# How the rows of w2 are split, how the last two output tiles are summed, and where scratch products stand, in a gated attention and MLP mix

## The chip, the core and the metric

The kernel runs on one core of a Trainium2 chip. The metric is the device time of one execution in microseconds (us), lower is better.

## What is computed

```python
def _A_ref(x, wqkv, wo):            # 16 heads of 28, S = 2048, D = 448
    qkv = ...                       # x @ wqkv, split into q, k, v
    idx = pos[:, None] - off[None, :]          # 8 keys: own position and 2, 4 .. 14 before
    logits = jnp.einsum("bhsd,bhswd->bhsw", q, kg) * scale
    attn = _softmax(masked logits, axis=-1)
    o = jnp.einsum("bhsw,bhswd->bhsd", attn, vg)
    return o.reshape(B, S, D) @ wo
def _B_ref(x, w1, b1, w2, b2):      # 448 -> 1792 -> 448, squared ReLU
    h = x @ w1 + b1
    r = jnp.where(h > 0, h, 0)
    return (r * r) @ w2 + b2
g = _sigmoid((x * gate_w).sum(-1, keepdims=True))
return g * a + (1 - g) * b
```

Everything is float32.

## The kernel before

**Precision.** TensorE (PE) works on a rounded 32-bit type. Every operand is therefore split into a high part (ScalarE, ACT, copies it into the rounded type) and a low part (VectorE, DVE, subtracts the high part from the raw value). Each product is the sum of three: high by high, high by low, low by high.

**Half rows.** The inner size 448 is 3 x 128 + 64. `side_by_side` issues products in pairs: one on rows 0 to 63 of the array, one on rows 64 to 127, for two different accumulators that lie in two PSUM banks. To sum all 128 rows of an operand, each accumulator first gets one half and later the other (`wo_first` and `wo_second`, `h_first` and `h_second`, `o_part` with `second`). Between the two, a tiny ACT instruction (`touch`, L702) makes sure that the first half has left PE. `qkv_first` (L403) is an exception: there the first products use all 128 rows, one slice k of x and wq at a time, for four token tiles.

**Stages.** (1) q, k and v for four chunks of 512 tokens, to 105 us. (2) The MLP in 28 turns of a loop over `g`: each computes two hidden tiles of 128 for one chunk (`h_first`, `h_turn`, `h_second`, `mlp_ops`) and adds the two hidden tiles before to the four token tiles' outputs (`o_part`). (3) The attention runs meanwhile on GpSimd (POOL: products, L506 and L518) and DVE (reductions, L510 and L528). (4) The heads' outputs times `wo`: pairs of token tiles, `wo_split` and then `wo_first` and `wo_second`; four pairs lie between the turns, four at the end, the last three of them in the final loop over `n`. `fin_add` (L991) takes an accumulator times its gate into the output tile and stores it (L995).

**Order of work.** Nothing is scheduled at run time. The order on ACT, DVE, POOL and SP (which issues the transfers) is written by a small planner (`Plan`): each job has a cost, dependencies and a priority, and is emitted when its turn comes in the plan's own time `plan.t`, which PE's products push on. START, FIRST, `plan.wire`, `plan.free` and the like set the plan's clock to the opening, which is written by hand. Accumulators in PSUM come from two rings of four, "m" (hidden tiles, attention outputs, copies of rows) and "b" (the MLP's outputs). `Acc` takes a place from a ring, and a later job gives it back.

**Rows of w2 and wo.** Rows 0 to 6 of w2 (128 x 448 each) are brought in before the loop. `row` loads the others and wo's: raw row to SBUF (L1109), high part on ACT (L1115). For the low part there are two ways. With `direct` DVE subtracts from the raw row in SBUF (L1117; the planner marks this job as using the port that DVE and POOL share). Without it the row waits in `rows_in` until `row_split` copies it with ACT into a PSUM bank of ring "m" (L1131) and DVE subtracts from there (L1133). Rows 7 to 10 go the first way, rows 11 to 13 and wo's the second, at most one in a turn.

**Scratch products.** `keep_warm(n)` (L774) issues n products of a zero tile into a bank that nobody reads: 16 ahead of everything, and after the first and second slices of `qkv_first` FILL[k] = 2 and 1 more.

Of the kernel before, what the change touches and what calls it, by code (L numbers as in the profile page):

```python
# [13 lines left out]
S, D, H, DH, W, F = 2048, 448, 16, 28, 8, 1792  # L14
P = 128
# [7 lines left out]
CH = 512  # L23
# [7 lines left out]
MM448, MM512 = 200.0, 226.7  # L31
PE_LAT = 175.0
LAT = 60.0
START = 4500.0
ORDER = (3, 0, 1, 2)
WARM = 16
FIRST = (3100.0, 2600.0, 2500.0)
FILL = (2, 1, 0)
PP_BUFS = 4
ST_BUFS = 3  # L40
BT_BUFS = 8
# [13 lines left out]
class Plan:  # L55
# [124 lines left out]
def gated_mix_kernel(ctx: ExitStack, tc: tile.TileContext, xT, wqkv, w1, w2, wo, b1, b2, out):  # L180
    nc = tc.nc

    def f32(ap):
        return ap.bitcast(F32)
# [60 lines left out]
    def dma(fn, packets, size, *deps, prio=MID, at=0.0):  # L245
        return add(SYNC, 430.0, fn, *deps, prio=prio, at=at, move=(packets, size))
# [147 lines left out]
    def qkv_first(x):  # L394
        four = range(4)
        q = accs(0, 0, four, "bbbb")
        for k in range(3):
            todo = [full(x, q[i], i, 0, (k,)) for i in four]
            for some in ((0, 1), (2, 3)) if k == 0 else (four,):
                for j in range(3):  # L400
                    for i in some:
                        acc, a, w, *_ = todo[i][j]
                        nc.tensor.matmul(acc.pt[:, :NQ], a, w, start=k == j == 0, stop=False)  # L403
            plan.pe(FIRST[k])
            keep_warm(FILL[k])
        for acc in q:
            acc.todo = 3
        k = accs(0, 1, four, "mmmm")
        t = [sum((last(x, a[i], i, b) for i in four), []) for b, a in ((0, q), (1, k))]
        f = [full(x, k[i], i, 1) for i in four]  # L410
        run(0, [t[0] + f[0] + f[1] + f[2] + f[3], t[1] + f[2] + f[3] + f[0] + f[1]],
            [(3, [(0, 0, q[0])], (k[0], k[0])),
             (12, [(0, i, q[i]) for i in (1, 2, 3)], (k[1], k[1])),
             (24, [], (k[0], k[2])), (33, [], (k[1], k[3])),
             (39, [(1, 0, k[0]), (1, 2, k[2])]), (48, [(1, 1, k[1]), (1, 3, k[3])])])
# [290 lines left out]
    def go(todo):  # L706
        side_by_side(*todo)
# [61 lines left out]
    nc.vector.memset(f32(zero), 0.0)  # L769
    nc.vector.memset(none, 0.0)  # L770

    def keep_warm(n):
        for _ in range(n):
            nc.tensor.matmul(warm[:, :2 * P].rearrange("p (i n) -> p i n", i=2), zero,  # L774
                             zero[:, None].to_broadcast([P, 2, P]), start=True, stop=True)

    keep_warm(WARM)

    raws = [rawp.tile([P, 4, 512], F32, tag="raw", name="wqraw0")]
    rx = rawp.tile([P, 4, 512], F32, tag="raw", name="xraw0")  # L780
    for cols in (slice(0, 256), slice(256, CH)):
        nc.scalar.dma_start(rx[:, 0, cols], xT[0, :, 0, cols])
    for k in range(4):
        if k < 3:
# [13 lines left out]
    x = X(x_tiles(0, xap))  # L798
    for k in range(3):
        nc.scalar.activation(wqh[:, k, :NQ], raws[0][:, k, :NQ], AF.Copy)  # L800
        for n, cols in enumerate((slice(0, 256), slice(256, CH)) if k == 0 else (slice(0, CH),)):
            if k or n:
                nc.scalar.activation(x.h[k][:, cols], rx[:, k, cols], AF.Copy)
            else:
                nc.vector.tensor_copy(x.h[k][:, cols], rx[:, k, cols])
            if not n:
                nc.vector.tensor_sub(wql[:, k, :NQ], raws[0][:, k, :NQ], f32(wqh[:, k, :NQ]))
            nc.vector.tensor_sub(x.l[k][:, cols], rx[:, k, cols], f32(x.h[k][:, cols]))
# [3 lines left out]
    nc.vector.tensor_sub(x.x8, rx[:, 3], f32(x.x7))  # L812


    plan.t, plan.wire = START, 17500.0
    plan.now = 10500.0
    plan.free.update({ACT: 11290.0, DVE: 11950.0, POOL: 1400.0, SYNC: 10500.0})
    raw_free[0] = raw_free[1] = [event(12000.0)]

    def wq_split(b, k):  # L820
        at = (11500.0, 13000.0)[b - 1]
# [7 lines left out]
    for k in range(4):  # L829
# [3 lines left out]
    xl = {1: x_load(1, 0), 2: x_load(2, 1)}  # L833
    w1_piece(1, None)
    x_bring(1, *xl[1], spill=False)
    x_stored[0] = [dma(lambda j=j, x=x: nc.sync.dma_start(x_d[0, j], f32(x.t[j])), 128, 4096, event(11950.0), prio=MID)
                   for j in range(4)]
    w1_piece(2, None)
    w1_piece(0, 0)
# [239 lines left out]
    def wo_three(acc, oh, ol, wh, wl, js):  # L1079
        return [(acc, oh, wh, js[0]), (acc, oh, wl, js[1]), (acc, ol, wh)]  # L1080

    def wo_full(st, r, ks):
        return sum((wo_three(st.accs[r], st.oh[:, k, r], st.ol[:, k, r], woh[:, k], wol[:, k], wo_jobs[k]) for k in ks), [])

    def wo_first(st):
        need(*st.jobs)
        go([wo_three(st.accs[r], st.o7, st.o8, wo7h, wo7l, wo_jobs[3]) + wo_full(st, r, (0, 1, 2)) for r in range(2)])
        j = touch(woh[:, 2, 0:1], plan.after_pe())
        for a in st.accs:
            a.rows, a.after = None, (j,)  # L1090

    def wo_second(st):
        go([wo_full(st, 1 - r, (2, 0, 1)) for r in range(2)])
        part_last[st.place] = [plan.after_pe()]
        for r in range(2):
            fin_add(st.par, st.t + r, st.accs[r], gt[:, st.par, st.t + r:st.t + r + 1])
# [43 lines left out]
    def w2_row(f):  # L1140
        name = f"w2raw{f}"
        row_low[name] = event()
        w2_jobs[f] = (row(name, w2[:, f], *w2hl(f), direct=f < NFA + 4), row_low[name])

    def wo_row(k):
        name = f"woraw{k}"
# [25 lines left out]
    def is_done(*jobs):  # L1172
        return all(plan.end(j) is not None and plan.end(j) < plan.t for j in jobs)
# [10 lines left out]
    for g in range(2, 2 * NF):  # L1184
        i, f = g // (NF // 2), g % (NF // 2) * 2
        c = ORDER[i]
        pc, pf = (c, f - 2) if f else (ORDER[i - 1], NF - 2)
        ends = f == NF - 2 and i < 3
        last = g == 2 * NF - 1
        if not f:  # L1190
            x, slots = X([nxt[j][0] for j in range(4)]), [nxt[j][1] for j in range(4)]
            x.parts = [(nxt[j][2], nxt[j][2]) for j in range(4)]
            nxt = {}
        if ends:
            plan.calm = plan.t + 21 * MM512 + 12 * MM448
        accs = h_first(x, c, f)
        if todo_rows:
            todo_rows.pop(0)()
        if f == 2 and 0 < i < 3:
            x_reload(i + 1, 3, free)  # L1200
        if ends:
            x_reload(i + 1, 0, slots[3])
        if last:
            wo_take(True)
        elif not todo_rows and not rows_in and len(wo_todo) + len(wo_loaded) > 4 and not wo_ready:
            wo_take()
        if f in (NF - 4, NF - 2):
            for tl in both:
                fin_fetch(c // 2, (c % 2) * 4 + tl)
        h_turn(accs, f)  # L1210
        if rows_in and is_done(rows_in[0][2]):
            row_split(*rows_in.pop(0))
        if g == 2:
            o_all(c, 0, True)
            del hs[c, 0], hs[c, 1]
        for tls in (left, right)[:1 if ends else 2]:
            o_part(pc, pf, False, tls)
        o_turn(pc, pf, left if ends else both)
        if f in (NF - 6, NF - 4):
            for tl in left if f == NF - 6 else right:  # L1220
                fin_begin(c // 2, (c % 2) * 4 + tl)
        h_second(x, accs, f)
        mlp_ops(accs, c, f)
        if ends:
            x_reload(i + 1, 1, slots[2])
            x_reload(i + 1, 2, slots[0])
            free = slots[1]
            o_part(pc, pf, False, right)
            o_turn(pc, pf, right)
        st = at_hand() if last or wo_ready else None  # L1230
        if st:
            wo_first(st)
            if last:
                wo_take(True)
        o_all(pc, pf, True)
        del hs[pc, pf], hs[pc, pf + 1]
        if st:
            wo_second(st)

    for n, (tls, second) in enumerate(((left, False), (right, False), (left, True), (right, True))):  # L1240
        if second:
            o_turn(c, f, tls)
        if n in (1, 2, 3):
# [51 lines left out]
```

## Time and profile before

| | |
|---|---|
| median of 3 runs | 416.26 us (416.22 to 418.59) |
| the profiled execution's own time | 417.06 us |
| its span, first to last instruction | 415.3 us |
| granted TensorE clock, mean | 0.998 |
| busy PE / DVE / ACT / POOL | 98% / 63% / 49% / 65% |
| moved by DMA | 73.75 MB, 178 GB/s on average |

Times in the views are microseconds from the start of the span. A row of the timeline has start, length, engine, line, operation, output and inputs, shape, the number of instructions that were merged in it, and, if the engine was idle before, for how long and what ended it. A row of a group has minimum, median and maximum of one instruction in ns. PE is matmul, PEld the loading of its weights, SPq the queue of SP. Matmuls overlap: one of 448 columns is shown 0.36 us long, but the next starts 0.2 us after it.

### The profile page before, as it was taken

The numbers are of one execution on the slowest core, as the hardware profiler recorded it, in microseconds if no ns is written. First come the engines' busy times: TensorE is split into PE (matmuls) and PEld (weight loads), VectorE is DVE, ScalarE is ACT, GpSimd is POOL, SyncE is SP. The second block draws the span as 40 slices with busy tenths as digits, with TensorE's granted clock in tenths as the row PEclk, the third lists the DMA queues.
The fourth block names the chain that finished last, engine by engine and source line by source line (L and its number), as shares of the span: only waits on it lengthen the run. The fifth ranks groups of instructions, "written<-read, shape, count | busy, mean of one in ns | idle before, by whom it ended". The sixth has DMA issues, their size and how long they took to land.

```text
span 415.3 us, 9283 instructions
## 1 busy us (share of the span) xinstructions
PE 408.8 (98%) x3847; PEld 376.7 (91%) x3847; DVE 263.3 (63%) x346; ACT 203.8 (49%) x497; POOL 270.2 (65%) x165
## 2 busy tenths in 40 slices
PE   8999999999999999999999999999999999999995
PEld 7999999999999988888888888988898888888994
DVE  4424422761486997877655998787786586493453
ACT  5657765332464655444455533543473343346730
POOL 0000000984989899989999897999899876950000
PEclk9999999999999999999999999999999999999999
DMA  7989999937164405544113668554626222057604
GB/s 235 393 285 318 371 367 357 377 112 252 46 219 182 149 11 226 208 142 170 38 48 127 203 149 291 160 138 138 194 70 220 108 86 83 1 148 156 144 2 177
DMA packets 64553, 73.75 MB, mean 178 GB/s; under 512 B 32320, under 2 KB 57344, under 8 KB 64128
## 3 DMA queue, kind: packets, MB, share of 16 engines
q1 hardware_dynamic: 64224, 72.90, 53.6%
q8 instruction: 30, 0.49, 0.5%
q10 hardware_dynamic: 288, 0.26, 0.2%
q14 instruction: 11, 0.09, 0.1%
HBM read 45.71 MB, written 28.25 MB: 178 GB/s over the span
## 4 chain that ended last, share of the span: by engine, by line
PE 94%; DVE 2%; issue 1%; DMA 1%; ACT 1%; DVEq 0%
PE b L316 30%; PE h L316 30%; PE qkv L316 23%; PE a L316 8%; PE qkv L403 2%; DMA wqraw<-wqkv 1%; DVE o L528 1%; DVE h L759 1%; DVE lg L510 0%; DVE w2bl L1117 0%; DVE bt_b L991 0%; ACT h L755 0%; ACT h L757 0%; DVEq L1290 0%; ACT wqh L800 0%
## 5 line engine op out<-in xcount | busy, mean ns | idle before, releaser
L506 POOL TENSOR_TENSOR pp<-q,k 128x896 f32<-128x896 f32 x64 | 139.1, 2208 | 83.4 <-DMA k<-k_d 77.5
L518 POOL TENSOR_TENSOR pp<-lg,v 128x896 f32<-128x896 f32 x64 | 119.4, 1959 | 5.4 <-DVE lg L510 4.6
L316 PE MATMUL qkv<-wqh,x 64*128 64x448 f32 (+1 forms) x528 | 91.6, 362 | 0.0
L510 DVE TENSOR_REDUCE lg<-pp 128x32 f32<-128x896 f32 x64 | 67.7, 1076 | 17.9 <-POOL pp L506 17.9
L316 PE MATMUL qkv<-wql,x 64*128 64x448 f32 (+1 forms) x264 | 75.2, 362 | 0.0
L316 PEld LDWEIGHTS qkv<-wqh,x 64*128 64x128 f32 x528 | 74.0, 184 | 0.3
L759 DVE TENSOR_TENSOR h<-h,h 128x512 fp32r<-128x512 f32 x56 | 38.6, 690 | 54.4 <-ACT h L758 53.7
L316 PE MATMUL b<-w2ah,h 64*128 64x448 f32 x448 | 69.2, 359 | 0.0
L528 DVE TENSOR_REDUCE o<-pp 128x112 f32<-128x896 f32 x64 | 67.1, 1067 | 2.1 <-POOL pp L518 2.1
L316 PE MATMUL b<-w2bh,h 64*128 64x448 f32 x448 | 66.8, 360 | 0.6 <-DVE h L759 0.6
L755 ACT ACTIVATE h<-h,b1z 128x512 f32<-128x512 f32 x56 | 36.6, 654 | 40.1 <-PE h L316 40.1
L316 PEld LDWEIGHTS b<-w2ah,h 64*128 64x128 f32 x448 | 47.2, 184 | 2.8
L316 PE MATMUL b<-w2al,h 64*128 64x448 f32 x224 | 46.9, 358 | 0.0
L316 PEld LDWEIGHTS b<-w2bh,h 64*128 64x128 f32 x448 | 42.1, 184 | 4.5 <-DVE h L759 0.9
L316 PEld LDWEIGHTS qkv<-wql,x 64*128 64x128 f32 x264 | 44.7, 184 | 0.2
L316 PE MATMUL b<-w2bl,h 64*128 64x448 f32 x224 | 40.7, 358 | 0.0
L338 ACT ACTIVATE st<-qkv 128x448 f32<-128x448 f32 x48 | 24.3, 539 | 22.8 <-PE qkv L316 15.5
L702 ACT ACTIVATE w1h<-w1h 128x2 fp32r<-128x2 f32 x28 | 5.8, 207 | 58.9 <-PE h L316 58.9
L757 ACT ACTIVATE h<-h 128x512 fp32r<-128x512 f32 x56 | 33.4, 596 | 1.5
L758 ACT ACTIVATE h<-h 128x512 f32<-128x512 f32 x56 | 33.2, 593 | 0.0
L316 PE MATMUL h<-x,w1h 64*128 64x512 f32 x168 | 33.0, 386 | 0.0
L316 PE MATMUL h<-x0b,w1h 64*128 64x512 f32 x168 | 28.1, 386 | 0.0
(129 smaller groups left out, 726.5 us busy)
## 6 DMA issues: line engine op xcount, KB each, us to landing
k<-k_d SPq DMA_DIRECT2D x8, 840.0 KB, 6.4
v<-v_d SPq DMA_DIRECT2D x8, 840.0 KB, 5.4
x_d<-x SPq DMA_DIRECT2D x12, 512.0 KB, 7.0
q_d<-st SPq DMA_DIRECT2D x8, 448.0 KB, 4.8
k_d<-st SPq DMA_DIRECT2D x8, 448.0 KB, 4.0
v_d<-st SPq DMA_DIRECT2D x8, 448.0 KB, 4.5
q<-q_d SPq DMA_DIRECT2D x8, 448.0 KB, 3.8
o_d<-o SPq DMA_DIRECT2D x16, 224.0 KB, 2.4
```

Of the source, the lines that this page charges most:

```text
L316: nc.tensor.matmul(acc.pt[:, :acc.n], a[rows], w[rows], start=acc.todo == acc.all, stop=acc.todo == 1)
L338: nc.scalar.activation(st[0][:, :, t % 2], pt[:, :D].rearrange("p (g c) -> p g c", g=G), AF.Copy)
L403: nc.tensor.matmul(acc.pt[:, :NQ], a, w, start=k == j == 0, stop=False)
L506: nc.gpsimd.tensor_mul(pr.rearrange("p (w c) -> p w c", w=W), q[:, s:s + 1].to_broadcast([P, W, C]), k[:, s:s + W])
L510: nc.vector.tensor_reduce(lgs[i][:, s], pr.rearrange("p (w h d) -> p w h d", w=W, h=HG), axis=AX.X, op=ALU.add)
L518: nc.gpsimd.tensor_mul(pr.rearrange("p (h d w) -> p w h d", h=HG, w=W), lgs[i][:, s][:, :, :, None].to_broadcast([P, W, HG, DH]), vs[i][:, ...
L528: nc.vector.tensor_reduce(o_t[par, s][:, g * C:(g + 1) * C], pr.rearrange("p (c w) -> p c w", w=W), axis=AX.X, op=ALU.add)
L702: return add(ACT, 205.0, lambda: nc.scalar.activation(ap, f32(ap), AF.Copy), *deps, prio=TURN)
L755: a = add(ACT, 656.0, lambda pt=pt, r=r: nc.scalar.activation(pt, pt, AF.Relu, bias=b1t[:, f + r:f + r + 1]), ready, bias_job[0], prio=NEXT)
L757: b = add(ACT, 600.0, lambda pt=pt, hh=hh: nc.scalar.activation(hh, pt, AF.Square), a, prio=NEXT)
L758: a = add(ACT, 600.0, lambda pt=pt: nc.scalar.activation(pt, pt, AF.Square), b, prio=NEXT)
L759: low = add(DVE, 690.0, lambda pt=pt, hh=hh, hl=hl: nc.vector.tensor_sub(hl, pt, f32(hh)), a, prio=NEXT)
```

## The change

All of w2's rows 7 to 13 now go by way of a PSUM copy. A turn of the loop may split two rows instead of one, and at g == 3 it splits two whether or not the plan has their high parts done. For the last pair of output tiles, `wo_first` sums only the 64-row slice (`wo7h`, `wo7l`), the MLP's part follows, and the new `wo_end` sums the three full slices with all 128 rows, all nine products of the first tile, its `fin_add`, then all nine of the second. The scratch products between the slices of `qkv_first` are gone, 18 instead of 16 stand ahead, and the plan's constants for the opening are set anew.

```diff
-START = 4500.0
+START = 4900.0
-WARM = 16
-FIRST = (3100.0, 2600.0, 2500.0)
-FILL = (2, 1, 0)
+WARM = 18
+FIRST = (2700.0, 2450.0, 2400.0)
...
             plan.pe(FIRST[k])
-            keep_warm(FILL[k])
...
-    keep_warm(WARM)
+    for _ in range(WARM):
+        nc.tensor.matmul(warm[:, :2 * P].rearrange("p (i n) -> p i n", i=2), zero,
+                         zero[:, None].to_broadcast([P, 2, P]), start=True, stop=True)
...
-    plan.t, plan.wire = START, 17500.0
-    plan.now = 10500.0
-    plan.free.update({ACT: 11290.0, DVE: 11950.0, POOL: 1400.0, SYNC: 10500.0})
-    raw_free[0] = raw_free[1] = [event(12000.0)]
+    plan.t, plan.wire = START, 15000.0
+    plan.now = 9800.0
+    plan.free.update({ACT: 10700.0, DVE: 11400.0, POOL: 1400.0, SYNC: 9800.0})
+    raw_free[0] = raw_free[1] = [event(11500.0)]
...
-    ... event(11950.0), prio=MID)          # stores of x_d[0, j]
+    ... event(11500.0), prio=MID)
...
-    def wo_first(st):
+    def wo_first(st, ks=(0, 1, 2)):
         need(*st.jobs)
-        go([wo_three(st.accs[r], st.o7, st.o8, wo7h, wo7l, wo_jobs[3]) + wo_full(st, r, (0, 1, 2)) for r in range(2)])
+        if not ks:
+            for a in st.accs:
+                a.all = a.todo = 12
+        go([wo_three(st.accs[r], st.o7, st.o8, wo7h, wo7l, wo_jobs[3]) + wo_full(st, r, ks) for r in range(2)])
...
+    def wo_end(st):
+        for r in range(2):
+            for e in wo_full(st, r, (0, 1, 2)):
+                acc, a, w, *js = e
+                need(*acc.after, *js)
+                nc.tensor.matmul(acc.pt[:, :D], a, w, start=False, stop=acc.todo == 1)
+                acc.todo, acc.after = acc.todo - 1, ()
+                plan.pe(MM448)
+            fin_add(st.par, st.t + r, acc, gt[:, st.par, st.t + r:st.t + r + 1])
...
-        w2_jobs[f] = (row(name, w2[:, f], *w2hl(f), direct=f < NFA + 4), row_low[name])
+        w2_jobs[f] = (row(name, w2[:, f], *w2hl(f), direct=False), row_low[name])
...
-        if rows_in and is_done(rows_in[0][2]):
-            row_split(*rows_in.pop(0))
+        for _ in range(2):
+            if rows_in and (g == 3 or is_done(rows_in[0][2])):
+                row_split(*rows_in.pop(0))
...
-            wo_first(st)
+            wo_first(st, (0, 1, 2) if n < 3 else ())
         o_part(c, f, second, tls)
-        if n in (1, 2, 3):
+        if n in (1, 2):
             wo_second(st)
+    wo_end(st)
```

More of the change, by code (lines that the diff above doesn't have):

```diff
@@ L770, in gated_mix_kernel @@
     nc.vector.memset(none, 0.0)
[L772 to L775, printed above, removed]
-    keep_warm(WARM)
+    for _ in range(WARM):
+        nc.tensor.matmul(warm[:, :2 * P].rearrange("p (i n) -> p i n", i=2), zero,
+                         zero[:, None].to_broadcast([P, 2, P]), start=True, stop=True)
     raws = [rawp.tile([P, 4, 512], F32, tag="raw", name="wqraw0")]
     rx = rawp.tile([P, 4, 512], F32, tag="raw", name="xraw0")
-    for cols in (slice(0, 256), slice(256, CH)):
+    halves = slice(0, 256), slice(256, CH)
+    for cols in halves:
         nc.scalar.dma_start(rx[:, 0, cols], xT[0, :, 0, cols])
@@ L800, in gated_mix_kernel @@
         nc.scalar.activation(wqh[:, k, :NQ], raws[0][:, k, :NQ], AF.Copy)
-        for n, cols in enumerate((slice(0, 256), slice(256, CH)) if k == 0 else (slice(0, CH),)):
+        for n, cols in enumerate(halves if k == 0 else (slice(0, CH),)):
             if k or n:
@@ L835, in gated_mix_kernel @@
     x_bring(1, *xl[1], spill=False)
-    x_stored[0] = [dma(lambda j=j, x=x: nc.sync.dma_start(x_d[0, j], f32(x.t[j])), 128, 4096, event(11950.0), prio=MID)
+    x_stored[0] = [dma(lambda j=j, x=x: nc.sync.dma_start(x_d[0, j], f32(x.t[j])), 128, 4096, event(11500.0), prio=MID)
                    for j in range(4)]
```

## The prediction, made before the changed kernel ran

> **What bounds the kernel now.** I read the page first, then the waits of PE, then the timeline around each place where PE is not full.
>
> ```profile
> span 415.3 us, 9283 instructions
> PE 408.8 (98%) x3847; PEld 376.7 (91%) x3847; DVE 263.3 (63%) x346; ACT 203.8 (49%) x497; POOL 270.2 (65%) x165
> PE warm L774 <- DVE b1z L770: 1.1, 1, 1.1
> PE b L316 <- DVE h L759: 0.6, 1, 0.6
> PE qkv L403 <- ACT wqh L800: 0.3, 1, 0.3
> ```
>
> The span is PE's: 408.8 of 415.3 us. The three last rows are all the waits of PE: one before its first instruction, one before the first real product, one in the MLP. Outside them an edit can move the time only if it takes instructions out of PE's stream, or shortens what follows PE's last product. So there are three places to price: the opening, the one stall in the middle, the end.
>
> **The opening: scratch products.** The list shows PE's products from the first one to the first that use half of the rows, with the operand work that could hold them.
>
> ```profile
> 1.06 3.54 PE L774 MATMUL warm<-zero 128*128 128x256 f32 x16 [1.06 <-DVE b1z L770]
> ...
> 3.58 0.63 PE L774 MATMUL warm<-zero 128*128 128x256 f32 x2
> 3.79 0.59 PE L774 MATMUL warm<-zero 128*128 128x256 f32 x2
> 4.21 0.40 PE L774 MATMUL warm<-zero 128*128 128x256 f32 x2
> 4.33 0.28 PE L774 MATMUL warm<-zero 128*128 128x256 f32 x1
> ...
> 4.29 0.58 ACT L800 ACTIVATE wqh<-wqraw 128x450 fp32r<-128x450 f32 x1 [1.34 <-DMA wqraw<-wqkv]
> 4.93 0.68 PE L403 MATMUL qkv<-wqh,x 128*128 128x450 f32 x2 [0.32 <-ACT wqh L800]
> 4.91 0.63 DVE L807 TENSOR_TENSOR wql<-wqraw,wqh 128x450 fp32r<-128x450 f32 x1
> 5.59 0.68 PE L403 MATMUL qkv<-wql,x 128*128 128x450 f32 x2
> ...
> 7.26 0.68 DVE L808 TENSOR_TENSOR x<-xraw,x 128x512 fp32r<-128x512 f32 x1
> 7.71 0.41 PE L774 MATMUL warm<-zero 128*128 128x256 f32 x2
> 7.96 0.97 PE L403 MATMUL qkv<-wqh,x 128*128 128x450 f32 x4
> 9.03 0.69 DVE L808 TENSOR_TENSOR x<-xraw,x 128x512 fp32r<-128x512 f32 x1 [0.25 <-ACT x L803]
> 10.37 0.28 PE L774 MATMUL warm<-zero 128*128 128x256 f32 x1
> 10.49 0.97 PE L403 MATMUL qkv<-wqh,x 128*128 128x450 f32 x4
> 12.12 0.98 PE L403 MATMUL qkv<-wqh,x 128*128 128x450 f32 x4
> 13.04 0.47 PE L316 MATMUL qkv<-w7h,x 64*128 64x450 f32 x2
> 13.35 0.37 PE L316 MATMUL qkv<-w7l,x 64*128 64x448 f32 x2
> ```
>
> Three scratch products go: two at 7.71, one at 10.37. The next real product starts at 7.96 and 10.49, so they hold the stream for 0.25 and 0.12 us. What would end a wait there if they were gone? The second slice's x remainder is split at 7.26 + 0.68 = 7.94; its high part was there before that split began, and the remainder is first read by the ninth of the slice's twelve products, 8 x 0.2 us after the first, at about 9.3. The third slice's remainder is ready at 9.72, before that slice starts at all. So nothing steps into the gap: **0.37 us gained**. If the remainder were needed first, the second slice could start no earlier than 7.94 and 0.12 would be left; I keep 0.12 as the lower bound.
>
> Two scratch products are added at the front. Before 4.2 us they start 0.21 apart (3.58, 3.79), at the end 0.12 apart (4.21, 4.33). The two new ones start at 4.45 and 4.57 and leave PE at 4.69, before the first weights at 4.29 + 0.58 = 4.87: cost nothing. Even if all were 0.21 apart, the first product would start at some 5.06 in place of 4.93; behind it only two products run (0.2 each) before PE has to wait for the weight remainder, at 4.91 + 0.63 = 5.54. That wait swallows 0.13. The cover is thus 5.59 - 5.33 = 0.26 us; beyond it each tenth counts.
>
> By the Trainium skill (TensorE: Matmul & The Clock Gate, Part 1) the slow spell is a window of about 3.4 us that runs freely and does not begin with the kernel, so its end may vary by about 0.5 us. This trace has one such end, near 4.2 us. By that rule a late end would make the whole opening of both kernels slower alike, and the sum would stay what it is to within the 0.13 us above.
>
> The constants of the plan (START, FIRST, the free times, the wire) move no time by themselves; they can change the order of SP's issues in the first 30 us. PE has no wait between 13.04 and 146 us, so whatever was queued there was early. I take zero and let a rival hold the rest.
>
> **The stall in the middle.** Here are PE, DVE, POOL and ACT around 141 us, the groups of L1117, and one stretch of the busy times (length, PE, PEld, DVE, ACT, POOL).
>
> ```profile
> 131.91 0.39 PE L316 MATMUL h<-x,w17h 64*128 64x512 f32 x1
> 141.47 0.39 PE L316 MATMUL h<-x,w17h 64*128 64x512 f32 x1
> 141.82 0.50 PE L316 MATMUL h<-x,w17h 64*128 64x512 f32 x2
> 146.26 0.47 PE L316 MATMUL b<-w2bh,h 64*128 64x448 f32 x2 [0.56 <-DVE h L759]
> 152.21 0.39 PE L316 MATMUL h<-x,w17h 64*128 64x512 f32 x2
> ...
> 134.10 6.31 POOL L506 TENSOR_TENSOR pp<-q,k 128x896 f32<-128x896 f32 x3
> 136.05 5.44 DVE L1117 TENSOR_TENSOR w2bl<-w2raw,w2bh 128x448 fp32r<-128x448 f32 x1
> 145.53 0.68 DVE L759 TENSOR_TENSOR h<-h,h 128x512 fp32r<-128x512 f32 x1
> 144.85 0.53 ACT L1131 ACTIVATE c_w2raw<-w2raw 128x448 f32<-128x448 f32 x1
> 147.12 0.61 DVE L1133 TENSOR_TENSOR w2bl<-c_w2raw,w2bh 128x448 fp32r<-128x448 f32 x1
> ...
> L1117 DVE TENSOR_TENSOR w2bl<-w2raw,w2bh x4: 608/1788/5436, 136.1 to 150.6; 128x448 fp32r<-128x448 f32 x4
> 141.50:152.20 10.70, 10.14 (x94) 9.13 (x92) 10.70 (x12) 6.18 (x13) 9.63 (x5) 1.00 0.01 2
> ```
>
> PE's product at 146.26 waits for DVE's L759, which ends at 145.53 + 0.68 = 146.21. That is late because DVE is busy all 10.70 us of this stretch, and the backlog began with L1117: a 128x448 subtraction that takes 0.61 us at best took 5.44, over exactly the time in which POOL runs its three products (134.10 to 140.41). DVE reading two SBUF tensors stood behind POOL.
>
> What is the stall worth? One turn of the MLP loop is 141.47 - 131.91 = 9.56 us; the next is 152.21 - 141.47 = 10.74, so the leading half of the rows loses 1.18 us. But the other half runs 141.82 - 141.47 = 0.35 behind, and after the stall both are in step (x2 at 152.21). The trailing half, which will end the kernel, loses 1.18 - 0.35 = 0.83.
>
> The change takes the four L1117 out and puts in four copies on ACT (0.53 each, 2.1 in all) and four subtractions from PSUM (0.61 each, 2.4 in all). L1133 already does this for other rows, at its normal length beside a busy POOL. DVE has one operand of SBUF less and no hold. ACT works 6.18 of 10.70 us in that stretch, so two copies of 0.53 in a turn find room; the copies end before the work of the next hidden tile asks for ACT. Behind them on ACT stands only the touch after the output products, and on DVE the reductions, which nobody on PE waits for. **0.83 us gained**; bounds 0 (another late subtraction takes the place) and 1.18.
>
> **The end.** PE's last product, the two last additions, the stores.
>
> ```profile
> 410.35 0.37 PE L316 MATMUL a<-woh,o 64*128 64x448 f32 x2
> 410.76 1.28 DVE L991 SCALAR_TENSOR_TENSOR bt_b<-a,zg,bt_b 128x448 f32<-128x448 f32 x2 [0.53 <-PE a L316]
> 411.47 0.92 SPq L995 DMA_DIRECT2D out<-bt_b  x2
> L995 SPq DMA_DIRECT2D out<-bt_b x12: 332/340/402, 272.2 to 412.1; - x12
> DMA to landing us min/median/max: 1.9/2.0/3.0
> ```
>
> Before, both last tiles end together at 410.73: two additions in a row, the second store issued at 412.1, about 2 us to land. After, the first tile ends nine products (1.8 us) earlier; its addition and store lie under the other nine. Only one addition and one store follow: the last store goes where the first went, 411.47 in place of 412.1, **0.6 us earlier**. The products cost the same: 18 pairs of half rows at 0.2 us become 18 of all rows at 0.2 us (12 products at L403 from 10.49 on took 2.4). The touch between the two kinds has the six pairs of o_part, 6 x 0.2 = 1.2 us, to hide it.
>
> Against that stands one more switch from half rows to all rows. The one switch the trace has, the other way, is at 13.04: the four products from 12.12 on are the last of the whole rows (at 0.2 us apart the last starts at 12.72), so the first pair would start at 12.92 and the second at 13.12; the second starts at 13.35, so **0.23 us lost**. Bounds 0.1 and 0.4. The end is worth 0.6 - 0.23 = 0.37.
>
> The Trainium skill (TensorEngine Tiling (Array Packing), Key Properties) says that changing the tiling mode drains the engine, which speaks against this edit. If a drain cost a whole product's tail, 0.36 - 0.2 = 0.16, and an uncovered weight load of 0.19, it would be 0.35, and the sum below 0.12 us less.
>
> **The sum.** 0.37 + 0.83 + 0.37 = 1.57 us. The profiled execution took 417.06 us, 1.76 of it outside the span of 415.3; it would take 415.5. It lies 0.8 above the median of the runs, 416.26; that goes to **414.7 us**, 0.4% faster. About 1% is what a measurement of this kernel can tell from no change, so the forecast itself falls within it.
>
> **Rivals.**
> 1. The halves stay out of step without cost, or the switch is free: 1.18 in the middle and 0.6 at the end give 2.15, so 414.1. For it: the leading half issues first. Against: the trailing half has the last word at each touch. Chance 0.11.
> 2. The gap in the middle only moves: DVE is full there and POOL, no longer stopped, brings its reductions sooner; or the new order at the opening costs as much later. The 0.83 is lost: 415.5. Against it: four subtractions shrink from up to 5.44 to 0.61. Chance 0.14.
> 3. Slower. The copies take PSUM buffers of the ring "m" (four), of which each turn's hidden tiles take two; now two copies a turn take the other two, and the next turn cannot start until their subtractions end. Today a copy at 144.85 is subtracted by 147.73 and the next turn starts at 152.21: 4.48 us of margin, less 0.53 + 0.61 for the second, 3.34. If DVE (or a row that lands late and is forced at g == 3) holds a subtraction for 5.44, PE waits 2.1 us; in one turn that gives 416.26 - 0.74 + 2.1 = 417.6, in three (two rows each at g = 3, 4, 5) 421.8. It decides from a delay of 3.34 us. Against: with L1117 gone nothing on DVE in this stretch stood for so long. Chance 0.10, most of the second kind.
> 4. The scratch products don't matter, something else holds the second slice: 0.12 in place of 0.37, so 414.95. Chance 0.08, inside the forecast's range.
>
> The forecast itself has 0.57. The range is 413.8 to 417.0: it takes in cases 1, 2 and 4 with 0.3 us on the fast side for the spread of runs, and leaves out the ring. Slower by over 1% is the case of three turns, 0.07; faster by over 1% would need 4 us where PE idles for less: 0.02; within 1%: 0.91.
>
> **What would show it.** Right: no scratch product after the first real one, first half-row product near 12.67; L1131 x11, L1133 x11 and no L1117; the turn from 141 to 151 us 9.56 long, no wait of PE for L759; the last two L991 about 1.8 us apart, one store after PE's end, span near 413.7. Wrong: PE waiting at the start of a hidden tile in g = 4 to 6, a gap of over 0.4 us before the last 18 products, or a stretch in the first 120 us in which PE waits for ACT's or DVE's x.

## The result, and the profile after

The changed kernel takes **415.92 us** (median of 14 runs, 415.59 to 416.46), the kernel before 417.02 in as many (416.22 to 418.59): a ratio of 0.9976, with an interval of 0.9966 to 0.9986. It is faster by about 1.1 us, inside the range, where 414.7 was forecast; and the interval, 0.1% to each side, does tell it from no change. The profiled execution took 415.95, with a span of 414.1. Lines of `kernel.py` have moved: L315 is the old L316, L402 the old L403, L504 the old L506, L757 the old L759, L771 the old L774, L987 the old L991, L991 the old L995, L1140 and L1142 the old L1131 and L1133; L1096 stands in the new `wo_end`.

The head of the page of the changed kernel, then all waits of PE (total, times, longest):

```profile
span 414.1 us, 9249 instructions
PE 408.6 (99%) x3828; PEld 404.2 (98%) x3828; DVE 258.6 (62%) x346; ACT 206.0 (50%) x501; POOL 265.8 (64%) x165
PE warm L771 <- DVE b1z L768: 1.1, 1, 1.1
PE qkv L402 <- ACT wqh L796: 0.3, 1, 0.3
```

The wait in the MLP, 0.6 us for DVE's L759, is gone. Its place in the timeline of the changed kernel, with the rows that are now split by way of PSUM, the lines L1140 and L1142, and the turn's busy times:

```profile
133.84 6.37 POOL L504 TENSOR_TENSOR pp<-q,k 128x896 f32<-128x896 f32 x3
135.17 1.00 ACT L1140 ACTIVATE c_w2raw<-w2raw 128x448 f32<-128x448 f32 x2
135.92 1.14 DVE L1142 TENSOR_TENSOR w2bl<-c_w2raw,w2bh 128x448 fp32r<-128x448 f32 x2
141.35 0.39 PE L315 MATMUL h<-x,w17h 64*128 64x512 f32 x1
150.91 0.39 PE L315 MATMUL h<-x,w17h 64*128 64x512 f32 x1
...
L1140 ACT ACTIVATE c_w2raw<-w2raw x7: 531/532/532, 135.2 to 163.9; 128x448 f32<-128x448 f32 x7
L1142 DVE TENSOR_TENSOR w2bl<-c_w2raw,w2bh x7: 608/616/627, 135.9 to 164.4; 128x448 fp32r<-128x448 f32 x7
141.40:150.95 9.55, 9.55 (x94) 9.55 (x92) 6.50 (x9) 6.33 (x14) 9.55 (x5) 1.00 0.01 3
```

Two subtractions take 1.14 us together beside the same three POOL products, where one took 5.44 before. The turn is 150.91 - 141.35 = 9.56 long, and DVE is busy for 6.50 of it, not all of it.

The opening (L402 are the products of all rows; the next first use half rows) and the end:

```profile
5.00 0.68 PE L402 MATMUL qkv<-wqh,x 128*128 128x450 f32 x2 [0.28 <-ACT wqh L796]
6.18 1.21 PE L402 MATMUL qkv<-wqh,x 128*128 128x450 f32 x4
6.23 0.42 ACT L799 ACTIVATE x<-xraw 128x256 fp32r<-128x256 f32 x1 [1.28 <-DMA xraw<-xT]
6.68 0.42 DVE L804 TENSOR_TENSOR x<-xraw,x 128x256 fp32r<-128x256 f32 x1 [0.74 <-ACT x L799]
7.63 1.36 PE L402 MATMUL qkv<-wqh,x 128*128 128x450 f32 x6
9.63 1.76 PE L402 MATMUL qkv<-wqh,x 128*128 128x450 f32 x8
11.23 0.96 PE L402 MATMUL qkv<-wql,x 128*128 128x450 f32 x4
12.03 0.96 PE L402 MATMUL qkv<-wqh,x 128*128 128x450 f32 x4
12.92 0.47 PE L315 MATMUL qkv<-w7h,x 64*128 64x450 f32 x2
...
405.79 0.37 PE L315 MATMUL b<-w2bl,h 64*128 64x448 f32 x2
406.09 0.47 PE L1096 MATMUL a<-woh,o 128*128 128x448 f32 x1
406.40 0.37 PE L1096 MATMUL a<-wol,o 128*128 128x448 f32 x1
408.20 0.68 DVE L987 SCALAR_TENSOR_TENSOR bt_b<-a,zg,bt_b 128x448 f32<-128x448 f32 x1 [0.73 <-PE a L1096]
409.60 0.37 PE L1096 MATMUL a<-woh,o 128*128 128x448 f32 x1
410.01 0.68 DVE L987 SCALAR_TENSOR_TENSOR bt_b<-a,zg,bt_b 128x448 f32<-128x448 f32 x1 [1.12 <-PE a L1096]
410.72 0.33 SPq L991 DMA_DIRECT2D out<-bt_b  x1
```

So the span can be cut into three stretches, and each step of the change is meant for one of them, but for the switch of rows at the end, which lies in the second: up to the first half-row product (before 13.04, after 12.92), from there to PE's end (410.72 - 13.04 = 397.68; 409.97 - 12.92 = 397.05), and from PE's end to the end of the span (415.28 - 410.72 = 4.57; 414.08 - 409.97 = 4.11). The gains are 0.12, 0.63 and 0.46: 1.21 in all. Every experiment below is read by these three numbers, called opening, middle and tail.

### The profile page after: what moved, and what is told of

Its sections match the earlier page's. It is cut to its first block, busy times and chain, and to the rows that moved or that the text cites. A ratio compares the mean times of both kernels' runs of the same rounds, so it can differ in the third digit from the quotient of the medians.

```text
span 414.1 us, 9249 instructions
## 1 busy us (share of the span) xinstructions
PE 408.6 (99%) x3828; PEld 404.2 (98%) x3828; DVE 258.6 (62%) x346; ACT 206.0 (50%) x501; POOL 265.8 (64%) x165
## 4 chain that ended last, share of the span: by engine, by line
PE 98%; DMA 1%; DVE 0%; ACT 0%; issue 0%
PE b L315 32%; PE h L315 32%; PE qkv L315 23%; PE a L315 7%; PE qkv L402 2%; PE a L1096 1%; DMA wqraw<-wqkv 1%; DVE bt_b L987 0%; ACT wqh L796 0%
## 5 line engine op out<-in xcount | busy, mean ns | idle before, releaser
L504 POOL TENSOR_TENSOR pp<-q,k 128x896 f32<-128x896 f32 x64 | 135.1, 2152 | 86.9 <-DMA k<-k_d 78.4
L315 PE MATMUL qkv<-wqh,x 64*128 64x448 f32 (+1 forms) x528 | 91.6, 362 | 0.0
L757 DVE TENSOR_TENSOR h<-h,h 128x512 fp32r<-128x512 f32 x56 | 38.7, 691 | 67.2 <-ACT h L756 66.8
L315 PE MATMUL b<-w2ah,h 64*128 64x448 f32 x448 | 78.8, 359 | 0.0
L315 PE MATMUL b<-w2bh,h 64*128 64x448 f32 x448 | 78.7, 359 | 0.0
L315 PE MATMUL qkv<-wql,x 64*128 64x448 f32 (+1 forms) x264 | 75.2, 362 | 0.0
L315 PEld LDWEIGHTS qkv<-wqh,x 64*128 64x128 f32 x528 | 74.0, 184 | 0.3
L315 PEld LDWEIGHTS b<-w2ah,h 64*128 64x128 f32 x448 | 63.8, 184 | 0.0
L315 PEld LDWEIGHTS b<-w2bh,h 64*128 64x128 f32 x448 | 62.9, 184 | 0.2
L315 PE MATMUL b<-w2al,h 64*128 64x448 f32 x224 | 63.1, 358 | 0.0
L315 PE MATMUL b<-w2bl,h 64*128 64x448 f32 x224 | 62.3, 358 | 0.0
L315 PEld LDWEIGHTS qkv<-wql,x 64*128 64x128 f32 x264 | 44.7, 184 | 0.2
L315 PEld LDWEIGHTS b<-w2al,h 64*128 64x128 f32 x224 | 38.4, 184 | 0.0
L315 PEld LDWEIGHTS b<-w2bl,h 64*128 64x128 f32 x224 | 37.7, 184 | 0.1
L315 PE MATMUL h<-x,w1h 64*128 64x512 f32 x168 | 35.7, 386 | 0.0
L315 PE MATMUL h<-x0b,w1h 64*128 64x512 f32 x168 | 35.6, 386 | 0.0
```

The costliest lines, as they stand in the source:

```text
L315: nc.tensor.matmul(acc.pt[:, :acc.n], a[rows], w[rows], start=acc.todo == acc.all, stop=acc.todo == 1)
L504: nc.gpsimd.tensor_mul(pr.rearrange("p (w c) -> p w c", w=W), q[:, s:s + 1].to_broadcast([P, W, C]), k[:, s:s + W])
L757: low = add(DVE, 690.0, lambda pt=pt, hh=hh, hl=hl: nc.vector.tensor_sub(hl, pt, f32(hh)), a, prio=NEXT)
```

## The experiments

Theory: three independent gains, of the scratch products (0.12 us each), of the hold of L1117 (0.83), and of the last addition and store (0.6, less 0.2 for a switch of rows). Rivals: the parts only work together, or the rest is chance of the execution.

### One part at a time

All rows by PSUM alone:

```diff
-        ... direct=f < NFA + 4), row_low[name])
+        ... direct=False), row_low[name])
-        if rows_in and is_done(rows_in[0][2]):
-            row_split(*rows_in.pop(0))
+        for _ in range(2):
+            if rows_in and (g == 3 or is_done(rows_in[0][2])):
+                row_split(*rows_in.pop(0))
```

> Before, with only the rows part of the change: rows 7 to 10 by way of the PSUM copy, up to two splits in a turn. Theory (the parts are independent, this one is worth what the trailing half lost): no wait of PE for the subtraction of hidden tiles near 146 us, the turn from 141 to 151 us is 9.56 us instead of 10.74 on the leading half, the span is 0.8 us shorter than before, the median 0.6 to 1.0 us below. Rival (the lead lost counts): 1.2 us. Rival (the gap only moves): a new wait of PE in the turns after, gain under 0.3 us.

Measured: 417.0 (before 417.24 beside it), ratio 0.9993 [0.9985, 1.0002]: no gain that the medians show, where 0.6 to 1.0 was expected. Opening 13.19, **middle 396.84**, tail 5.15. PE no longer waits for L759, and the middle is 0.84 shorter, as reckoned. The tail took back 0.58 and the opening 0.15. From the issue of the last store (411.38) to the end of the span it is 3.8 us, where the kernel before has 415.28 - 412.06 = 3.2:

```profile
411.38 0.33 SPq L995 DMA_DIRECT2D out<-bt_b  x1
```

The data has landed in the same 1.9 us; the 0.58 is spent in the last instructions of the program: 0.45 of it from the landing to SP's last drain (0.72 instead of 0.27), the rest in GpSimd's instructions behind that. Why they are late isn't shown.

The end alone (`wo_end`, `ks` of `wo_first`, and the last loop as in the full change):

> Before, with only the end changed: the last two output tiles one by one, all rows. Theory: the switch from half rows to all rows costs PE 0.2 us, the last store is issued 0.4 us earlier after that, the span is 0.3 to 0.4 us shorter; the time to the span's end after the last store stays 3.2 to 3.4 us, so a tenth of this may go either way. Rival (one store alone lands later than the second of two, which would explain 0.14 us of the changed kernel): 3.4 us or more behind the last store here too, gain 0.25 us or less.

Measured: 416.88, ratio 0.9993 [0.998, 1.0005], again no gain that the medians show. Opening 13.07, middle 398.29, **tail 3.94**. The tail is 0.63 shorter, as reckoned (0.6), with 3.2 us behind the last store, so the rival failed. The middle is longer by 0.61. Of that 0.20 is the switch; 0.42 is this pause, for x that is brought in again:

```profile
324.30 0.19 PEld L316 LDWEIGHTS h<-x2b,w1h 64*128 64x128 f32 x2 [0.55 <-DMA x2b<-x_d]
```

It came in this and three other kernels' profiles, for x1b or x2b (waits of 0.2 to 0.5 us), and not in those of before and after. That it is chance, and not of this edit, is likely by that, but not shown.

The opening alone, with the plan's new constants:

```diff
-START = 4500.0
-WARM = 16
-FIRST = (3100.0, 2600.0, 2500.0)
-FILL = (2, 1, 0)
+START = 4900.0
+WARM = 18
+FIRST = (2700.0, 2450.0, 2400.0)
+FILL = (0, 0, 0)
...        (wire, now, free times and two events as in the full change)
```

> Before, with only the opening changed: 18 scratch products ahead, none between the slices, the plan's constants as in the changed kernel. Theory (the first slice waits for the second half of x to land, which varies from run to run by some 0.4 us; the products taken out are worth 0.37 us): the half rows begin 0.37 us earlier than in an opening of the old form in which x's second half landed at the same time: 12.67 with x's second half at 5.8 us, 12.92 with 6.2. Median 0 to 0.4 us below before. Rival (the missing scratch products themselves make the slices slower, by clock or by a wait): products of the second and third slice more than 0.21 us apart, or half rows not before 12.9 us although x's second half landed at 5.8.

Measured: 418.22, ratio 1.0022 [1.001, 1.0033]: **slower**, by more than the noise. Opening 13.40, middle 398.89, tail 4.56. Two things went against the expectation. PE's clock was full only from 7.28 us in this execution (4.20 before), so that the first real products ran at half speed. And the wait for L759 more than doubled (another wait, of 0.5 us for a part of the attention's output before the last products, is new as well):

```profile
PE b L316 <- DVE h L759: 1.4, 1, 1.4
136.42 5.35 DVE L1117 TENSOR_TENSOR w2bl<-w2raw,w2bh 128x448 fp32r<-128x448 f32 x1
142.69 0.61 DVE L1117 TENSOR_TENSOR w2bl<-w2raw,w2bh 128x448 fp32r<-128x448 f32 x1
144.22 0.68 DVE L759 TENSOR_TENSOR h<-h,h 128x512 fp32r<-128x512 f32 x1
144.81 0.98 DVE L1117 TENSOR_TENSOR w2bl<-w2raw,w2bh 128x448 fp32r<-128x448 f32 x1
```

The new constants put DVE's work into another order around L1117. The prediction's "move no time by themselves" failed here, where the four L1117 keep DVE full.

Rows and end together, with the old opening:

> The changed kernel with before's opening (16 scratch products ahead, 2 and 1 between the slices, the old constants): rows and end alone. Theory (parts add): span 1.2 us shorter than before, within 0.2 us of the changed kernel if x's second half lands as there, median 0.9 to 1.3 us below before. Rival (the parts interact, the opening's order of transfers matters later): a new wait of PE between 13 and 146 us, or a sum that differs from the single parts by over 0.3 us.

Measured: 416.25, ratio 0.9971 [0.996, 0.9982]. Opening 13.13, middle 397.34 (0.3 of it a pause for x1b), tail 4.11. Two parts that were worth nothing measurable alone give all of the change's gain together. By the stretches each had earned its own part alone too; the late end of the program (and 0.15 of the opening) took it back in the first, the switch and the pause in the second. How many executions have the pause the medians don't show. The tail is 4.11 or 4.12 in every profile that has both parts, except in two where one more thing is changed below (3.98 and 4.53).

### What holds L1117, and what replaces it

Only row 7 by PSUM, still one split in a turn and none forced:

```diff
-        ... direct=f < NFA + 4), row_low[name])
+        ... direct=NFA < f < NFA + 4), row_low[name])
```

> Before, with only row 7 of w2 by way of the PSUM copy; rows 8 to 10 are still subtracted from SBUF. Theory (whichever subtraction of two SBUF operands starts while POOL has its chain of products is held for as long as the chain): row 8 is held in row 7's place for 4 to 5.5 us near 136 us, DVE stays full from 136 to 152 us and PE's wait for L759 stays between 0.4 and 1.5 us; PE from the first half-row product to its end 397.5 to 398.5 us, as before (397.68). Rival (only the first row of the four meets POOL): no L1117 over 2.1 us, no wait of PE, 396.85 us as with all four rows moved.

Measured: 420.91 (before 416.61), ratio 1.0106 [1.0092, 1.012]. The hold behaves as expected: the next row in line, row 8, is now held for 5.4 us. But the time went the other way, which nothing in the expectation had: row 7's low part was made a turn too late.

```profile
L1117 DVE TENSOR_TENSOR w2bl<-w2raw,w2bh x3: 608/1977/5401, 136.1 to 147.7; 128x448 fp32r<-128x448 f32 x3
PE b L316 <- DVE w2bl L1133: 2.8, 2, 2.2
147.83 0.19 PEld L316 LDWEIGHTS b<-w2bl,h 64*128 64x128 f32 x2 [2.61 <-DVE w2bl L1133]
148.55 0.59 PE L316 MATMUL b<-w2al,h 64*128 64x448 f32 x2
148.92 0.59 PE L316 MATMUL b<-w2ah,h 64*128 64x448 f32 x2
152.05 0.41 PE L316 MATMUL h<-x,w1l 64*128 64x512 f32 x2
```

PE's weight loads stood for 2.61 us and its products for 2.2; from 148.55 the products start 0.37 apart and more, until 152.05. The granted clock is half from 148.53 to 151.95. The whole is a middle of 402.1.

The changed kernel, without the forced splits at `g == 3`:

```diff
-            if rows_in and (g == 3 or is_done(rows_in[0][2])):
+            if rows_in and is_done(rows_in[0][2]):
```

> The changed kernel, but a row is split at the third group's turn only if it is already there by the plan (the 'g == 3 or' is taken out); two splits a turn as in the changed kernel. In the order of DVE rows 7 and 8 are then split one turn later. Theory (the forced turn is what keeps the split ahead of the products that read it): PE waits for DVE's L1142 once near 145 us for 2.6 to 3.2 us, the products behind it run at half clock for about 3.4 us more (1.7 lost), PE's stretch 401 to 402, median 419.5 to 421. Rival (two a turn catch up, so the split is in time): no wait for L1142, 397.05, median as the changed kernel's.

Measured: 419.97 (before 416.87), ratio 1.0078 [1.0065, 1.009]; opening 12.69, middle 401.11. The time is what theory said, its anatomy is not. Not one long wait and a slow clock, but four short ones, a turn apart (145 to 177 us), at full clock; for the weight loads they add up to 3.9 us:

```profile
PE b L315 <- DVE w2bl L1142: 2.4, 4, 0.6
145.07 1.16 DVE L1142 TENSOR_TENSOR w2bl<-c_w2raw,w2bh 128x448 fp32r<-128x448 f32 x2 [0.60 <-ACT c_w2raw L1140]
145.74 0.47 PE L315 MATMUL b<-w2bl,h 64*128 64x448 f32 x2 [0.59 <-DVE w2bl L1142]
```

So the part of the diff that looks like a detail carries the change. The copies in PSUM free DVE, but here they pay only when they are made one turn earlier; without that the detour costs 4 us where the hold cost 0.83.

### The scratch products and the opening

Eight and four scratch products behind the first two slices instead of two and one (the kernel before with `FILL = (8, 4, 0)`):

> Before with 8 and 4 scratch products between the slices in place of 2 and 1 (nine more). Theory (nothing waits there, each holds PE's stream for 0.12 us): the second slice starts 0.7 us later, the third 1.1 us later than before relative to the end of the first slice, half rows begin near 14.1 to 14.3 us, median 1.0 to 1.2 us above before. Rival (the slices wait for operands, scratch products fill idle time): less than 0.5 us later. If the first holds, the 0.37 us for three products was sized rightly, and what ate it in the changed kernel lies ahead of the second slice.

Measured: 418.24 (before 416.61), ratio 1.0045 [1.0033, 1.0058]; opening 14.38, middle 397.62.

```profile
7.91 1.12 PE L774 MATMUL warm<-zero 128*128 128x256 f32 x8
8.87 0.98 PE L403 MATMUL qkv<-wqh,x 128*128 128x450 f32 x4
11.34 0.64 PE L774 MATMUL warm<-zero 128*128 128x256 f32 x4
11.81 0.98 PE L403 MATMUL qkv<-wqh,x 128*128 128x450 f32 x4
```

8.87 - 7.91 = 0.96 for eight and 11.81 - 11.34 = 0.47 for four: 0.12 us each, so nine more account for 1.08. The opening is 14.38 - 13.04 = 1.34 longer; 0.15 of the rest is that the first product starts later (5.08 instead of 4.93), and the slices run a little slower. Theory held, with opening and median a little above their ranges (14.38 for 14.1 to 14.3, a median 1.6 above for 1.0 to 1.2).

None behind them, 18 ahead, old constants (the kernel before with `WARM = 18` and `FILL = (0, 0, 0)`):

> Before with 18 scratch products ahead and none between the slices, but the plan's old constants. Theory (the constants changed the order on DVE, and that made the wait in the middle 1.4 us where only the opening was changed): the wait of PE for L759 is 0.5 to 0.6 us again, PE from first half-row product to its end 397.7 us, half rows at 12.7 to 13.4 us by the time at which full clock is granted; median 0 to 0.4 us below before. Rival (the products taken out themselves make the later stage slower): the wait is over 1 us here too and the median 0.5 us or more above before.

Measured: 416.1 (before 416.61), ratio 0.9989 [0.9979, 0.9999]; **opening 12.66**, middle 397.07, tail 4.56. The opening came out where the prediction had it, at 12.67. And the wait in the middle vanished, which neither theory nor rival had, though L1117 is still there. Below are the rows of this kernel, and last the row of POOL that follows the three products in the kernel before:

```profile
133.59 6.79 POOL L506 TENSOR_TENSOR pp<-q,k 128x896 f32<-128x896 f32 x3
135.68 2.71 DVE L1117 TENSOR_TENSOR w2bl<-w2raw,w2bh 128x448 fp32r<-128x448 f32 x1
L1117 DVE TENSOR_TENSOR w2bl<-w2raw,w2bh x4: 1558/2064/2705, 135.7 to 149.1; 128x448 fp32r<-128x448 f32 x4
...
140.38 0.62 POOL L570 TENSOR_TENSOR lg<-lg,sm 128x256 f32<-128x256 f32 x1
```

Here DVE got in during POOL's three products, which took 6.79 instead of 6.31: less the 0.61 of its own work, it ran from 138.39 - 0.61 = 137.78, when the second product (135.67 to 137.90) ended. Before, it ran from 136.05 + 5.44 - 0.61 = 140.88, behind the third product and also behind the short L570; the prediction's "exactly the time" of the three products is too short, DVE stood until POOL had nothing more to run.

What differs is when L1117 comes up: 0.01 us behind the start of POOL's second product here, 0.14 ahead of it before. The 23 subtractions of this kind in the six profiles that have them sort the same way. Five met no POOL product (0.61 us). Five came up 0.01 to 0.14 us ahead of the start of POOL's next product, and stood until POOL ran dry (5.35 to 5.45 us in all). The other 13 came up 0.4 us or more ahead of it, and stood until the product that was running ended (0.92 to 2.71 us in all). Starts on POOL are rough, so that the tenth of a microsecond decides is read from the pattern, not shown. The stall of before is thus not certain either. The runs of the kernel before fit that: most lie between 416.2 and 417.4; whether the shorter ones are those without the stall isn't shown, as none of them has a profile.

By the Trainium skill (SBUF — State Buffer, "SBUF: two separate sides") the two engines share one pair of ports as an exclusive lock, which the one that starts first holds for its whole instruction. The 2.71 agrees with that; the 5.44 goes beyond it, for there the waiting engine was passed over between instructions of POOL.

x's second half brought by SP ahead of the second weights, in the changed kernel:

```diff
-    for cols in halves:
-        nc.scalar.dma_start(rx[:, 0, cols], xT[0, :, 0, cols])
+    nc.scalar.dma_start(rx[:, 0, halves[0]], xT[0, :, 0, halves[0]])
...
+            if not k:
+                nc.sync.dma_start(rx[:, 0, halves[1]], xT[0, :, 0, halves[1]])
```

> The changed kernel with the second half of x's first slice issued by SP right behind the first weights, ahead of the second slice's weights, in place of by ACT. Theory (the first slice waits for that half): its split starts at 5.0 to 5.4 us in place of 5.4 to 6.2, the first slice ends without a gap, half rows begin 0.1 to 0.3 us earlier for the same start of full clock, median 0 to 0.3 us below the changed kernel (415.92). Rival (the later weights now land late, or the clock sets the pace): no gain, second slice starts later than 8.0 us.

Measured: 416.8, ratio 1.0004 [0.9996, 1.0013], slower than the changed kernel with its 0.9976; opening 13.55, middle 397.07, tail 4.53. x's second half is split at 5.35 instead of 6.23, but the second slice's x lands later: "PE qkv L402 <- ACT x L800: 0.8, 1, 0.8". The rival held: the second slice starts at 8.55, and the order of the transfers only chose which operand came late.

Rows and end, with 18 scratch products ahead and none behind and the **old** constants:

> All rows of w2 by PSUM, the last two tiles one by one, 18 scratch products ahead of the first product and none behind it, but with the plan's old constants. Theory (each scratch product behind the first real one holds PE's stream for 0.12 us; the new constants only cost, since they bring the store of x and the reloads into another order and x's second half lands later): the first half-row product starts near 12.67 (0.25 to 0.4 earlier than in the kernel before with 13.04), PE from there to its end 397.05 as in the changed kernel (plus 0.3 if the reloaded x is late once), 4.1 from PE's end to the end of the span: span 413.8, median 0.2 to 0.4 below the changed kernel's. Rival (the opening is set by when the clock becomes full and when x lands, both by chance of the execution): half rows from 12.9 to 13.1, median equal to the changed kernel's within 0.2.

The changed kernel once more:

> The changed kernel once more, unchanged: a second profile and a median of the same chip as the others. Theory (clock and landing of x vary from execution to execution): the clock is full from a time other than 3.92 and the first half-row product starts anywhere in 12.7 to 13.4, while PE's stretch behind it stays 397.05 (plus 0.3 to 0.4 if reloaded x is late) and the tail 4.1. Rival (the opening is fixed by the program): half rows again at 12.92 within 0.05.

Measured: 415.9 (ratio 0.9978 [0.9968, 0.9988]) and 415.89 (0.9977 [0.9968, 0.9986]), before 416.87. Middle 397.05 and tail 4.11 in both, as in the first profile; openings 12.91 and 13.35. With the old constants the rival held (12.91 where 12.67 was expected, and a median no lower), with the changed kernel once more the theory. So the constants are worth nothing once L1117 is gone, and the fastest of all versions that were tried cannot be told from the change. The second profile of the same program starts its half rows 0.43 later, and its products of all rows run slower:

```profile
5.48 0.68 PE L402 MATMUL qkv<-wqh,x 128*128 128x450 f32 x2 [0.21 <-ACT wqh L796]
11.61 0.99 PE L402 MATMUL qkv<-wql,x 128*128 128x450 f32 x4
12.44 0.98 PE L402 MATMUL qkv<-wqh,x 128*128 128x450 f32 x4
13.35 0.47 PE L315 MATMUL qkv<-w7h,x 64*128 64x450 f32 x2
```

The first weights landed 0.47 later (first product at 5.48, against 5.00).

Six scratch products ahead instead of 18, in the changed kernel (`WARM = 6`):

> The changed kernel with 6 scratch products ahead of the first product instead of 18, so that PE is idle from about 2.4 to 4.9 us. Theory (the clock is full only after a stretch of a few us in which PE works): the first products start 0.4 apart, the clock is full only from 7 to 8.5 us, the first half-row product starts 1.5 to 2.5 later (14.4 to 15.4), median 417.5 to 418.5. Rival (the clock's window runs freely and any work in it will do): full near 4 to 7, half rows 12.9 to 13.4, median within 0.4 of the changed kernel's.

Measured: 417.54, ratio 1.0021 [1.0012, 1.0031], so 1.65 us more than the changed kernel beside it (415.89). Opening 15.34, middle 397.05, tail 4.12.

```profile
1.06 1.65 PE L771 MATMUL warm<-zero 128*128 128x256 f32 x6 [1.06 <-DVE b1z L768]
5.04 1.12 PE L402 MATMUL qkv<-wqh,x 128*128 128x450 f32 x2 [2.33 <-ACT wqh L796]
8.95 2.33 PE L402 MATMUL qkv<-wqh,x 128*128 128x450 f32 x6
```

The six products from 8.95 on still start 0.36 apart on average (the next is at 11.12); the granted clock is full only from 10.99, later than expected. Theory held in time and opening: without the twelve scratch products the real ones ran at the slow clock.

## Why the prediction was right or wrong, point by point

The mechanisms in the middle and at the switch held, and their sizes too. What failed are the last step of the sum (the base, 0.8 us), the opening's term (0.37 reckoned, 0.12 measured), a part of the end's term, and the sentence that about 1% is the least that can be told from no change.

**The middle: right.** 0.83 was reckoned. The middle fell by 0.84 with the rows alone, and by 0.63 in the full change, which is 0.83 less the 0.20 of the switch; the turn is 9.56 long and no product waits for L757. The cover that was named (ACT's room for two copies) held. What the prediction did not see is on what the gain depends: on the forced splits (4 us worse without), and on a stall that need not happen (absent in the profile of one kernel that still has L1117).

**The switch: right.** The last half-row pair starts at 405.79, the first whole products at 406.09 and 406.40: 0.29 and 0.31 instead of 0.20 and 0.20, 0.20 lost in all, against 0.23 reckoned. The Trainium skill (TensorEngine Tiling (Array Packing), Key Properties) has the engine drained at such a change. A delay is there, as a drain would make it; its price is 0.20 and not the 0.35 that the prediction estimated for a drain.

**The end: the term was mis-sized in the full program.** 0.6 was reckoned for one addition and one store less. Counted from PE's end, the last store is issued at 410.72 - 409.97 = 0.75 instead of 412.06 - 410.72 = 1.34: 0.59 earlier, and the end alone shortened the tail by 0.63. In the full change the tail fell by 0.46: from the issue of the last store to the end of the span it takes 3.36 instead of 3.22. What stands behind the last store was taken as fixed; it is not (3.2 to 3.8 us over these programs). Its cause wasn't settled.

**The opening: the term was mis-sized, though its price per product was right.** 0.37 was reckoned, 0.12 came in the profile. Each scratch product does cost 0.12 (0.96 for eight), and two kernels without any reached 12.66 and 12.69, where 12.67 was said. "Nothing steps into the gap" held as well: the products from 7.63 to 11.23 start 0.20 apart, over both places where scratch products had stood. The failed step is that everything ahead of the gaps was taken as equal in both kernels, though nobody had seen a second execution. In the changed kernel x's second half was split at 6.23 instead of 5.79, and the first slice stood for it: two products 0.31 and 0.32 apart, 0.23 lost. The first product started at 5.00 instead of 4.93, another 0.07. In other executions the clock (full from 3.92 to 7.28 over all that have the full number of scratch products) or the first weights were late. The five profiles with scratch products as before start their half rows at 13.04 to 13.19, the six without any, 18 ahead and the old order of x's transfers at 12.66, 12.69, 12.91, 12.92, 13.35 and 13.40: on average 13.11 and 12.99, a gain of 0.12 with a spread of 0.74. The lower bound of the prediction, 0.12, was the better value, by chance and not for its reason; so was rival 4, with the same 0.12 and a second slice that nothing held. Whether the medians hold any gain of the opening stays open: 0.9971 without it and 0.9976 with it have overlapping intervals.

**The clock.** The Trainium skill (TensorE: Matmul & The Clock Gate, Part 1) has the window of about 3.4 us run freely. The ends of the slow spell, 3.92 to 7.28 us, are 3.36 apart, and two of them are of one program (3.92, 5.30): the traces agree with that, and not with the half microsecond that the page gives for the spread of the end. The same page asks for an idle window of about 3.4 us before the clock falls; here a wait of 2.2 us (2.6 between weight loads) was enough to lose it for 3.4, and one of 1.4 (1.7) was not.

**The base: wrong.** The sum was made against 417.06, which gives 415.5; then it was moved down by 0.8 to the median of three runs, 416.26. With 14 runs that median is 417.02, and the profiled execution was a typical one. This step alone makes 0.8 of the 1.2 by which 414.7 missed; the other 0.4 are the opening (0.25) and the end (0.14), which leaves the middle and the switch right to 0.03. Three runs, of 416.22 to 418.59, could not carry a correction of 0.8; later sets of 21 to 31 runs of the kernel before have medians of 416.61 to 417.24. If the two short ones of the three were executions without the stall, which isn't shown, the sum even took the stall off twice.

**"About 1%": wrong.** The prediction put its own 0.4% below what can be told from no change. No run shows 1%: the intervals here reach 0.08% to 0.14% to each side, and the change's 0.24% lies clear of them.

**The other rivals.** None came true as written. That of the ring "m" (slower by a late row) did not happen in the change; but with one condition removed it nearly did, through the products that read the row and not through the ring.

## What to carry to other kernels

Split a span at the same products in both kernels and compare the stretches: here two parts looked worthless by their medians, while each had earned what it should and lost it elsewhere. A detour that frees a full engine pays only if it is begun early enough for the one who reads its result, so look at the reader's turn before the writer's cost. And do not correct a sum by a median of three runs when the spread of those runs is larger than the sum.

## What the runs showed of the hardware

- DVE's subtraction of two SBUF tensors took 0.61 us alone, up to 2.71 when it got in behind the POOL product that was running (2.1 us and more each), and 5.35 to 5.45 when it came up 0.01 to 0.14 us ahead of POOL's next product and stood until POOL ran dry; from PSUM it took 0.61 beside the same products.
- A change from pairs of half rows to whole rows on PE cost 0.20 us, in both directions alike (0.29 and 0.31 between starts instead of 0.20, at 13 and at 406 us).
- PE's products of all rows and 450 columns run in two rates at full clock: 0.200 apart in the first profile of the changed kernel (12.03 - 11.23 for four), 0.207 in the second (12.44 - 11.61). It lasts until the first half rows. The kernel before shows both in one profile, the slower from the fourth product behind the third slice's scratch product on, and so do the four other profiles with the same scratch products. Its cause isn't known.
